# Leaving out a doubled load and moving 24 loads further back in SyncE's queue: a linear-attention block followed by a gated MLP on one core

## The chip, the cores and the metric

The kernel runs on one core of one Trainium2 chip. The metric is the device time of one execution in microseconds; the time before is the median of three runs.

## The reference

Two blocks follow one another. The first is a linear attention with a decaying state, for 4 batches, 8 heads, 768 tokens and 48 channels a head; the second is an MLP on the joined heads (3072 tokens, 384 channels, 2048 hidden).

```python
f = 1.0 / (1.0 + np.exp(-f_logit))
for t in range(S):
    state = f[:, :, t, :, None] * state + np.einsum('bhd,bhe->bhde', k[:, :, t], v[:, :, t])
    y[:, :, t] = np.einsum('bhd,bhde->bhe', q[:, :, t], state)
x = y.transpose(0, 2, 1, 3).reshape(B * S, H * D)
h = x @ w_in
g = h * (1.0 / (1.0 + np.exp(-1.702 * h)))
out = g @ w_out
```

## The kernel before

**Units.** The tokens are worked off in 12 units of 256 tokens (three units to a batch), numbered 0 to 11; "the third unit" is number 2. For each unit the kernel computes scores in six levels (distances of 1, 2, 4, ... 32 tokens inside chunks of 64), masks them into the tile A, forms the products y of A with v (line 543), adds the products of q with the carried state (line 698), copies y to yT, and lets SyncE (SP) rearrange it by DMA into xT (lines 762 and 767), the input of that unit's MLP. Between levels, f, q and k are multiplied together in the tile X (lines 528 and 532, VectorE), and ScalarE sets copies aside in Kc and Qc (lines 503 and 509). The state is updated by VectorE (lines 673 to 677), after which the products of line 698 can go on.

**Loading f, q and k.** All three have one buffer each, in the tile raw, which is used again by every unit. `load_raw(n, j)` loads f (j = 0), q (1) or k (2) of unit n. For units 0 and 1 (N_FILL is 2) it issues four loads (line 280), and the turning into X and F is done by TensorE. From unit 2 on each of f, q and k is eight DMAs (line 287), four of 96 KB and four of 80 KB, and VectorE turns them (line 354). `begin_f`, `begin` and `begin_k` turn f, q and k of a unit; `begin_f` takes a list of pieces for units 0 and 1. v is loaded by `load_v` in five DMAs (lines 306 and 311), issued in the step that forms the state of the unit before.

**Weights.** The MLP's weights are fetched in 16 pairs of 768 KB (line 208, tile bits; w_in in two DMAs, w_out in one) into three buffers in turn, and converted in steps: one activation of ScalarE (line 239) and three VectorE operations (lines 235, 228 and 238). Pairs 0, 1, 4, 5, 8, 9, 12 and 13 are w_in, the others w_out. The fetch of pair n is issued when pair n - 3 has been converted, so it waits for that pair's buffer.

**Order.** TensorE's and GpSimd's instructions stand in the order in which they are written, and up to the end of `follow(2, ...)` so do all the others. `opening()` runs unit 0 with a first part of unit 1 inside it. `parts_of(n)` gives the parts of unit n, with the beginnings of unit n + 1 put between them; `follow` goes through them and, after each, emits a planned number of MLP products, conversion steps and other chores. For unit 1 the parts are six of scores ("W"), two turnings of k ("T"), the state ("S"), its products with q ("W"), and then the beginnings of unit 2 ("B", three times). The MLP products (line 1110 for h, line 1124 for o) fill TensorE between the parts.

**SP's queue.** All loads and stores but the first four of q are issued by SP, in one order. The DMAs use eight completion semaphores in turn, so a DMA is issued only when the one eight before it has landed.

Of the kernel before, what the change touches and what calls it, by code (L numbers as in the profile page):

```python
# [23 lines left out]
def kernel(  # L24
# [52 lines left out]
    N_FILL = 2  # L77
# [32 lines left out]
    def keep_up(times, columns=(NL - 1) * 64, of=None):  # L110

        if times:
            pt = bank([P, columns], f"idle_{next(serial)}")
        for _ in range(times):
            lhs, rhs = of or (ident, masks.rearrange("p l f t -> p (l f t)"))
            nc.tensor.matmul(pt, lhsT=lhs, rhs=rhs, start=True, stop=True)
# [10 lines left out]
    R = U // 32  # L127
# [131 lines left out]
    def load_raw(n, j, engines=(nc.sync,)):  # L259
        if n >= NALL:  # L260
            return
        b, s0 = n // NU, n % NU * U
        src = (f_logit, q, k)[j]
        first = s0 - (j == 1)

        def span(head, token, dims, d=0):
            return bass.AP(src.tensor, src.offset + ((b * H + head) * S + token) * D + d, dims)
        if n < N_FILL:
            for a in range(NP):
                engine = engines[a * len(engines) // NP]  # L270
                to = by_pair[j][32 * a:32 * (a + 1), :, :R * D]
                if first < 0 and a == 0:

                    for r, rows in ((1, 16), (17, 15)):
                        engine.dma_start(
                            out=to[r:r + rows], in_=span(0, r * R - 1, [[R * D, rows], [S * D, 2], [1, R * D]])
                        )
                    engine.dma_start(out=to[:1, :, D:], in_=span(0, 0, [[R * D, 1], [S * D, 2], [1, (R - 1) * D]]))
                else:
                    engine.dma_start(out=to, in_=span(2 * a, first, [[R * D, 32], [S * D, 2], [1, R * D]]))  # L280
            return
        for f in (1, 0):
            for r in range(4):
                lo = 32 * (r % 2)
                width = R4 * D - lo
                part = span(r // 2, first + (0 if f else HALF), [[R4 * D, 32], [2 * S * D, NP], [1, width]], lo)
                nc.sync.dma_start(out=by_half[32 * r:32 * (r + 1), j, f, :, :width], in_=part)  # L287
            if f and first < 0:
                for r in range(4):
                    lo = 32 * (r % 2)  # L290
                    nc.sync.dma_start(
                        out=by_half[32 * r:32 * r + 1, j, f, :, :D - lo],
                        in_=q[b - 1, r // 2::2, S - 1:S, lo:].rearrange("a t d -> t a d"),
                    )
# [33 lines left out]
    def attention(n):  # L328
# [11 lines left out]
        parts = []  # L340
# [7 lines left out]
        def turn(j, outs, fn=None, pieces=None):  # L348

            if n >= N_FILL:  # L350
                for f in (1, 0):
                    out = outs(f)
                    at, step = (0, 1) if f else (HALF - 1, -1)
                    nc.vector.transpose(  # L354
                        view(out, at, [[HALF, NP], [step, R4], [R4 * step, 32]]),
                        by_half[:, j, f].rearrange("p a (j d) -> p (a j) d", j=R4)[:, :, :32],
                    )
                if fn:
                    fn()
                return  # L360
            for j0 in pieces or range(0, R, 4):
                pt = bank([P, 4, P], f"t_{n}_{j}_{j0}")
                for jj in range(4):
                    for h in range(2):
                        x = (j0 + jj) * D
                        nc.tensor.matmul(
                            pt[h * HS:(h + 1) * HS, jj, :], lhsT=by_pair[j][:, h, x:x + HS], rhs=ident, start=True, stop=True
                        )
                for f in (1, 0):
                    at, step = (j0, 1) if f else (HALF - 1 - j0, -1)  # L370
                    nc.scalar.activation(
                        view(outs(f), at, [[HALF, NP], [R * step, 16], [step, 4]]),
                        pt.rearrange("p j (a f i) -> p f a i j", a=NP, f=2)[:, 1 - f],
                        (AF.Tanh if n > 1 else AF.Sigmoid) if fn else AF.Copy, scale=0.5 if fn and n > 1 else 1.0,
                    )
            if fn and n > 1:
                half_up()
# [9 lines left out]
        def begin_f(pieces=None):  # L387
            def decay():
                turn(0, lambda f: F[:, ORDER.index(f) * SLOT:(ORDER.index(f) + 1) * SLOT], sigmoid, pieces)
            if n > N_FILL + 1 and "moved" in copied:  # L390
                with tc.issue_after(copied["moved"].ins):
                    decay()
            else:
                decay()
            if n >= N_FILL or (n == 1 and R - 4 in pieces):
                load_raw(n + 1, 0)

        def begin():
# [359 lines left out]
        def to_x(y, x, ng, hs=range(2)):  # L758

            for h in hs:  # L760
# [3 lines left out]
                while at < D:  # L764
# [5 lines left out]
                    at += w  # L770

        return (begin_f, begin, begin_k, begin_gates), parts, (open_level, open_evacuate, turn_k), lambda: reverse_v(n)


# [415 lines left out]
    def parts_of(n):  # L1190

        parts = list(units[n][1])
        _, inter = parts.pop()
        if n and n != N_FILL:
            kind, scores = parts[0]
            _, ahead = units[n - 1][1][-1]
            def both():
                rest = ahead()
                scores()
                if rest:  # L1200
                    rest()
            parts[0] = kind, both
        if n + 1 < NALL:
            begin_f, begin, begin_k, begin_gates = units[n + 1][0]
            i = len(parts)
            if n + 1 < N_FILL:

                parts.append(("K", lambda: (begin_k(), begin_gates())))
                kind, head = parts[0]
                parts[0] = kind, lambda: (head(), load_raw(n + 1, 1), keep_up(1))  # L1210
                parts.insert(4, ("B", lambda: (begin(), load_raw(n + 1, 2))))
                parts.insert(2, ("B", begin_f))
            else:
                kind, states = parts.pop()
                if n in CARRY:
                    parts += [("B", begin_f), ("B2", begin), ("S1", lambda: (states(), begin_gates())), ("K3", begin_k)]
                elif n < N_FILL:
                    second = parts[1][1]
                    parts[1] = parts[1][0], lambda: (second(), [load_raw(n + 1, j) for j in range(3)])
                    def own():  # L1220
                        rest = inter()
                        rest()
                    parts += [(kind, states), ("W", own), ("B", begin_f), ("B", begin), ("B", lambda: (begin_gates(), begin_k()))]
                else:
                    parts += [("B", begin_k), (kind, lambda: (states(), begin_gates()))]
                    parts.insert(i - 3, ("B", lambda: (begin_f(), begin())))
        else:
            parts.append(("W", inter))
        return parts

    def merge(n, fill, columns, share):

        parts = parts_of(n)
        total = sum(share(kind) for kind, _ in parts)
        at = done = 0
        columns += state["behind"]
        for kind, fn in parts:
            while kind in ("S", "S1") and any(in_y.get(m) for m in range(n)):
                w, emit, _ = fill.pop(0)
                emit()  # L1240
                done += w
            fn()
            at += share(kind)
            end = max(done, columns * at / total)
            while fill and done < end:
                w, emit, _ = fill.pop(0)
                emit()
                done += w
        state["behind"] = max(0, columns - done)
# [139 lines left out]
```

## Time and profile before

| | |
|---|---|
| median of three runs | 596.62 us (595.42 to 597.95) |
| span of the profiled execution | 594.2 us |
| the profiled execution's own time | not given apart from its span; the median lies 2.4 us above the span |
| TensorE (PE) busy | 566.1 us, 95% |
| VectorE (DVE) busy | 435.9 us, 73% |
| ScalarE (ACT) busy | 300.0 us, 50% |
| GpSimd (POOL) busy | 136.2 us, 23% |
| mean granted TensorE clock | 0.983 |
| DMA | 61.05 MB, mean 103 GB/s |
| loads of f of 96 KB (line 287) | 52, of 80 KB 44, the doubled load included |

The busy shares are averages over the whole span. The first 110 us, in which unit 0 and unit 1 run and the weights arrive, are the only part where the DMA load is high, where TensorE has gaps, and where its granted clock falls to half for a time; what a step there is worth is read from timelines and short windows of that part. "SPq" rows are SP's DMA issues, with the time that the issues took and not the time of the transfers.

### The profile page before, as it was taken

The page shows a single profiled execution, that of the slowest core. Times are in us where ns is not written, and L with a number is a line of the kernel's source. Part 1 is how long each engine was busy: PE and PEld are TensorE (multiplying, and loading weights), DVE is VectorE, ACT ScalarE, POOL GpSimd, SP SyncE. Part 2 cuts the span into 40 slices and gives each one's busy share as a digit, 9 for nine tenths or more (in the row PEclk, how much of TensorE's full clock was granted, in tenths as well). Part 3 has the DMA queues.
Part 4 walks back from the last instruction along what each step waited for, and adds up shares of the span by engine and source line. Part 5 has one row for each costly group of instructions (what it writes and reads, how often), then busy time and mean ns, then how long its engine had stood idle before and what let it go on. Part 6 is the DMA issues. An engine that isn't in the chain of part 4 may idle for free.

```text
span 594.2 us, 18511 instructions
## 1 busy us (share of the span) xinstructions
PE 566.1 (95%) x7820; PEld 516.0 (87%) x7820; DVE 435.9 (73%) x697; ACT 300.0 (50%) x610; POOL 136.2 (23%) x226
## 2 busy tenths in 40 slices
PE   6869897999999999999999999999999999999997
PEld 5757574768789999999999999999999999998997
DVE  2887678985979777798787797786887786461284
ACT  4854534325452575474474574563663564553440
POOL 4020020145226610610600700700600601203000
PEclk9959899999999999999999999999999999999999
DMA  7879977434452543343452243453352111001000
GB/s 186 207 183 195 242 194 180 132 79 97 115 149 60 128 110 82 93 118 98 120 137 59 76 117 86 117 147 62 93 141 63 45 55 29 28 3 27 28 1 27
DMA packets 87923, 61.05 MB, mean 103 GB/s; under 512 B 33633, under 2 KB 79617, under 8 KB 87841
## 3 DMA queue, kind: packets, MB, share of 16 engines
q1 hardware_dynamic: 87504, 59.48, 40.0%
q8 instruction: 61, 1.00, 0.7%
q10 hardware_dynamic: 337, 0.39, 0.3%
q14 instruction: 21, 0.17, 0.1%
HBM read 46.21 MB, written 8.91 MB: 93 GB/s over the span
## 4 chain that ended last, share of the span: by engine, by line
PE 81%; DVE 6%; DMA 5%; issue 3%; ACT 2%; SPq 2%; POOL 0%; DVEq 0%; ACTq 0%; POOLq 0%
PE h L1016 17%; PE o_Y L878 13%; PE o_Z L878 9%; PE h L1110 8%; PE h_y L1016 6%; PE sc L434 6%; PE o L1124 5%; PE o_X L878 5%; PE o_W L878 4%; PE y L698 2%; PE y L543 2%; SPq L287 2%; PE sc L652 2%; DMA bits<-in_moe_w_in_dram 1%; DMA raw<-in_q_dram 1%
## 5 line engine op out<-in xcount | busy, mean ns | idle before, releaser
L532 DVE TENSOR_TENSOR X<-X,tot 128x1024 f32<-128x1024 f32 x50 | 66.0, 1319 | 42.6 <-PE sc L434 38.7
L503 ACT COPY Kc<-X 128x512 f32<-128x512 f32 x72 | 48.2, 670 | 71.0 <-DVE X L532 60.1
L978 POOL TENSOR_TENSOR E<-xT 128x128 f32<-128x128 f32 (+1 forms) x36 | 18.6, 526 | 235.4 <-DMA xT<-yT 204.8
L1110 PE MATMUL h<-xT,w_in 128*128 128x256 f32 x288 | 67.2, 390 | 3.9 <-DMA xT<-yT 1.9
L1110 PEld LDWEIGHTS h<-xT,w_in 128*128 128x128 f32 x288 | 55.0, 194 | 14.0 <-issue 3.1
L1016 PE MATMUL h<-E,w_in 128*128 128x128 f32 (+1 forms) x476 | 62.5, 277 | 0.3 <-DVE g L1044 0.3
L1016 PEld LDWEIGHTS h<-E,w_in 128*128 128x128 f32 x476 | 57.3, 192 | 1.0 <-issue 0.4
L878 PE MATMUL o_Y<-T,S 128*128 128x192 f32 x320 | 57.6, 329 | 0.0
L1046 ACT ACTIVATE g<-g 128x512 f32<-128x512 f32 (+1 forms) x70 | 40.3, 589 | 26.6 <-DVE g L1044 26.6
L878 PEld LDWEIGHTS o_Y<-T,S 128*128 128x128 f32 x320 | 52.3, 190 | 0.5
L712 ACT COPY yT<-y 48x256 f32<-48x256 f32 x88 | 32.3, 367 | 31.8 <-PE y L698 30.7
L1044 DVE TENSOR_TENSOR g<-g,h 128x512 f32<-128x512 f32 (+1 forms) x58 | 36.2, 639 | 15.1 <-PE h L1016 14.1
L1124 PE MATMUL o<-w_out,g 128*128 128x384 f32 x128 | 46.6, 515 | 0.0
L354 DVE STREAM_TRANSPOSE X<-raw 128x512 f32<-128x512 f32 x40 | 42.3, 1113 | 3.1 <-PE y L698 2.7
L494 DVE COPY_PREDICATED A<-masks,sc 128x256 f32<-128x256 uint32 (+1 forms) x98 | 42.0, 505 | 0.0
L1124 PEld LDWEIGHTS o<-w_out,g 128*128 128x128 f32 x128 | 25.1, 202 | 15.8 <-issue 2.3
L434 PE MATMUL sc<-X,Kc 48*64 48x64 f32 x1344 | 30.2, 228 | 4.7 <-DVE s L228 2.3
L434 PEld LDWEIGHTS sc<-X,Kc 48*64 48x64 f32 x1344 | 25.8, 142 | 9.1 <-ACT Kc L503 4.5
L1035 ACT ACTIVATE g<-h 128x512 f32<-128x512 f32 (+1 forms) x52 | 28.5, 576 | 9.9 <-PE h L1016 9.6
L1114 ACT ACTIVATE g<-h 128x256 f32<-128x256 f32 x48 | 17.7, 382 | 30.6 <-PE h L1110 30.4
L878 PE MATMUL o_X<-w_out,g 128*128 128x192 f32 x160 | 29.9, 332 | 0.5 <-ACT o_X L842 0.5
L1044 DVE TENSOR_TENSOR g<-g,h_y 128x512 f32<-128x512 f32 (+1 forms) x29 | 18.6, 641 | 14.9 <-PE h_y L1016 10.4
(161 smaller groups left out, 1173.5 us busy)
## 6 DMA issues: line engine op xcount, KB each, us to landing
bits<-in_moe_w_out_dram SPq DMA_DIRECT2D x8, 768.0 KB, 5.4
raw<-in_f_logit_dram SPq DMA_DIRECT2D x52, 96.0 KB, 2.2
raw<-in_k_dram SPq DMA_DIRECT2D x48, 96.0 KB, 3.0
bits<-in_moe_w_in_dram SPq DMA_DIRECT2D x8, 576.0 KB, 6.1
raw<-in_q_dram SPq DMA_DIRECT2D x44, 96.0 KB, 2.3
k_tok<-z SPq DMA_DIRECT2D x64, 64.0 KB, 1.8
kt<-k_tok SPq DMA_DIRECT2D x16, 256.0 KB, 2.9
out_dram<-osb SPq DMA_DIRECT2D x20, 192.0 KB, 1.9
```

Source lines behind the costliest of these rows:

```text
L354: nc.vector.transpose(view(out, at, [[HALF, NP], [step, R4], [R4 * step, 32]]), by_half[:, j, f].rearrange("p a (j d) -> p (a j) d", j=R4) ...
L434: nc.tensor.matmul(t["sc"][h][g * HS:(g + 1) * HS, a, s, :], lhsT=t["Kc", l][rows(h), x:x + HS], rhs=rhs(h, a, g), start=True, stop=True,)
L494: moved = nc.vector.copy_predicated(out=view(A, c * HALF + at, dims), mask=mask.bitcast(U32), data=got)
L503: nc.scalar.copy(c.rearrange("p (n two m) -> p n two m", two=2, m=m), view(X, KF * SLOT, [[2 * m, SLOT // (2 * m)], [(KR - KF) * SLOT + m, ...
L532: nc.vector.tensor_tensor(x, x, y, ALU.mult)
L712: nc.scalar.copy(view(yT[rows(h)], at, [[U, NP], [step, HS]]), py[columns(h, g), g, :, f, :])
L878: nc.tensor.matmul(t[name], lhsT=lhs(f), rhs=rhs(f), start=(new and i == 0), stop=(i == HF - 1), skip_group_check=True,)
L1016: nc.tensor.matmul(ph[:, t], lhsT=WA[a][:, f * P:(f + 1) * P], rhs=E[n][b], start=(root and t == 0), stop=not goes_on, skip_group_check=True,)
L1044: nc.vector.tensor_tensor(to, to, part, ALU.add if sign > 0 else ALU.subtract)
L1046: nc.scalar.activation(to, to, AF.Gelu_apprx_sigmoid)
L1110: nc.tensor.matmul(ph, lhsT=w_in[:, c, ff * P:(ff + 1) * P], rhs=xTs[n][:, c, :], start=(c == 0), stop=(c == NK - 1))
L1124: nc.tensor.matmul(t["po"], lhsT=g[ff // FG][:, ff % FG, tt * P:(tt + 1) * P], rhs=w_out[:, ff, :], start=(ff == ffs[0]), stop=(ff == ffs[ ...
```

## The change

In the kernel before, `begin_f` of unit 1 issues the load of f of unit 2 once the second of its two pieces is turned, inside `opening()`; and `parts_of(1)` issues f, q and k of unit 2 again behind the second scores of unit 1. Unit 2's f is thus loaded twice into the same place, with the same data. The change takes the condition for unit 1 out of `begin_f`, and hangs the three loads to the fifth scores of unit 1.

```diff
             else:
                 decay()
-            if n >= N_FILL or (n == 1 and R - 4 in pieces):
+            if n >= N_FILL:
                 load_raw(n + 1, 0)
...
                 elif n < N_FILL:
-                    second = parts[1][1]
-                    parts[1] = parts[1][0], lambda: (second(), [load_raw(n + 1, j) for j in range(3)])
+                    fifth = parts[4][1]
+                    parts[4] = parts[4][0], lambda: (fifth(), [load_raw(n + 1, j) for j in range(3)])
```

On SP eight DMAs fall away, and the fetches of weight pairs 6 and 7 stand ahead of the 24 loads of f, q and k of unit 2 instead of behind them. The order on the other four engines is the same in both kernels.

## The prediction

> **What bounds the kernel now.** I read the page first, then the chain that ended last, the timelines of SP, PE and DVE from 14 to 100 us, PE's waits, and busy time with granted clock in short windows. The page gives TensorE's busy share and clock in 40 slices:
>
> ```profile
> PE   6869897999999999999999999999999999999997
> ...
> PEclk9959899999999999999999999999999999999999
> ```
>
> PE is full from the eighth slice on, so a microsecond won or lost before about 109 us reaches the end; from there to the end PE's waits in the waits view come to some 5 us. The change acts between 21 and 76 us, where PE has gaps and the clock falls to half. There SP's queue issues every load in one order. SP's timeline (start, duration, line, destination<-source, count):
>
> ```profile
> 21.32 6.84 SPq L287 DMA_DIRECT2D raw<-in_f_logit_dram  x8
> ...
> 32.02 1.05 SPq L208 DMA_DIRECT2D bits<-in_moe_w_out_dram  x1
> ...
> 41.10 7.19 SPq L287 DMA_DIRECT2D raw<-in_f_logit_dram  x8
> 48.42 4.91 SPq L287 DMA_DIRECT2D raw<-in_q_dram  x8
> 53.44 3.70 SPq L287 DMA_DIRECT2D raw<-in_k_dram  x8
> 57.23 0.90 SPq L208 DMA_DIRECT2D bits<-in_moe_w_out_dram  x2
> 58.22 6.19 SPq L208 DMA_DIRECT2D bits<-in_moe_w_in_dram  x4
> 64.50 0.39 SPq L306 DMA_DIRECT2D vt<-in_v_dram  x1
> 64.93 5.41 SPq L311 DMA_DIRECT2D vr<-in_v_dram  x4
> 70.81 0.52 SPq L762 DMA_DIRECT2D xT<-yT  x1
> ...
> 73.69 0.53 SPq L762 DMA_DIRECT2D xT<-yT  x1
> ```
>
> The load of the third unit's f is there twice, at 21.32 and 41.10; q and k follow, and only at 57.23 the two w_out fetches for weight pairs 6 and 7. Behind them come pairs 8 and 9 (58.22), the next v, and at 70.81 the rows of xT that the MLP of the second unit needs. DVE and PE, same columns:
>
> ```profile
> 62.00 0.56 DVE L235 TENSOR_SCALAR a<-bits 128x768 int32<-128x768 uint32 x1 [1.84 <-DMA bits<-in_moe_w_out_dram]
> ...
> 76.02 2.02 DVE L354 STREAM_TRANSPOSE F<-raw 128x512 f32<-128x512 f32 x2
> ```
>
> ```profile
> 39.99 2.90 PE L1110 MATMUL h<-xT,w_in 128*128 128x256 f32 x6 [1.91 <-DMA xT<-yT]
> ...
> 67.95 1.24 PE L698 MATMUL y<-X,st 48*48 48x64 f32 x58 [2.05 <-issue]
> 69.12 6.92 PE L1124 MATMUL o<-w_out,g 128*128 128x384 f32 x16
> 76.46 9.30 PE L1110 MATMUL h<-xT,w_in 128*128 128x256 f32 x42 [0.42 <-issue]
> ```
>
> DVE waits 1.84 us for pair 6. PE waits 1.91 us for the first xT and 2.05 us ahead of the y products; its products h at 76.46 start just after the xT row block issued at 73.69 can have landed (2.8 us later). Last the clock: PE busy, the third number PEld, the number behind POOL the granted clock.
>
> ```profile
> 31.20:44.80 13.60, 8.92 (x152) 7.18 (x153) 11.52 (x19) 6.84 (x14) 2.37 (x5) 0.50 0.77 191
> ...
> 68.80:72.10 3.30, 3.30 (x19) 1.94 (x8) 1.22 (x2) 2.73 (x8) 0.00 (x0) 0.50 1.24 183
> ```
>
> ```profile
> 65.40:68.70 3.30, 1.25 (x60) 0.93 (x62) 3.09 (x9) 1.17 (x2) 0.00 (x0) 1.00 1.03 226
> ...
> 27.80:31.20 3.40, 1.58 (x70) 1.31 (x68) 3.26 (x7) 2.79 (x8) 1.75 (x2) 1.00 0.90 169
> ```
>
> The clock is half after each stretch of 3.4 us in which PE was busy less than half of the time (1.25 of 3.30, 1.58 of 3.40), and it came back at 44.9 only after a full stretch.
>
> **Part 1, the first load of f goes.** Eight DMAs (four of 96 KB, four of 80 KB, 704 KB) and 6.84 us of SP's time. The order of instructions on PE, DVE, ACT and POOL is the same in both kernels; SP loses these eight and nothing else. At the 235 GB/s of the window 21 to 32 us they are 3.0 us of transfer. Who was behind them: v for the second unit (29.42), then pair 3 (32.02). Pair 3 cannot be issued earlier, since it waits for a buffer that DVE's L228 frees at 31.7; but it took 5.9 us to land, against 4.74 for the same size at 57.23 (chain view). So the xT rows behind it come up to 1.2 us earlier. Nothing is added, so no loss: bounds 0 and 1.2, I take 0.8. That start lies at half clock until 44.9, so it is worth half: **-0.4 us** (0 to -0.6). PE then runs without a wait to 59.5, so it is passed on.
>
> **Part 2, 24 loads move behind the fifth scores.** Moved past on SP: the fetches of pairs 6 and 7, nothing else; POOL issues none. Those fetches then wait only for their buffers, freed by DVE's L228 at 46.3 and 50.1. They go out there instead of at 57.23 and 57.71 and land by about 52 and 56 at 5.9 us each, before DVE asks at 60.1. Removed: DVE's 1.84. What is late next is ACT, which prepares the pair between two copies: kn ends at 60.72, the activation takes 0.93, L228 0.56, L238 0.96, so the pair is done at 63.2 instead of 64.55. The states behind it, and the y products, come 1.3 us earlier: with part 1 at 66.2 instead of 67.95.
>
> That gain meets the xT rows, which stand last in SP's queue. In the new order the raw loads start at about 50.2 (50.1 plus 0.4 for pair 7, less 0.4). Before they took 16.0 us (41.10 to 57.13). The floor is k's own pace, 3.70 for 8, so 11.1 for 24. The ceiling is 16.0 again. Of the old time, f's 7.2 held waits for pairs 4 and 5: eight transfers are in flight at once, each issue waiting for the one eight before. In the new order only f's last two stand eight behind pairs 6 and 7; I give f 4.7 (3.7 and 1.0 of that wait), q and k their old 8.7: 13.4, nearer to the floor's side because pairs 4 and 5 have landed. They end at 63.6. Pairs 8 and 9 then need 1.3 and 0.8 with gaps, so v goes out at 65.9 instead of 64.50: **+1.4** (floor -0.9, ceiling +4.0). The transfers weigh against that: the DMA share is 1.05 from 57 to 72 us, the bytes from 39 us to xT are the same in both orders, and pairs 6 and 7 now fill time before 57. Half-way, I take **+0.6** for xT, so h starts at 77.1 instead of 76.46 and the 1.7 us won at y are gone.
>
> The raw loads themselves: k lands about 66, its first reader is behind F's transposes at 76.02, ten microseconds of cover. Without it each late microsecond would be one of PE.
>
> The Trainium skill, "DMA: Bandwidth & Descriptors", section "Rules for kernel authors", says to issue a DMA early and wait for it late. It speaks against moving these loads; the trace agrees only that there is a wait to lose, and by this rule alone nothing is lost until the ten microseconds of cover are used up.
>
> Then the clock. PE's o products start at 67.5 and need 6.9 us at mostly half clock, 5.2 at full (4.68 for 14 at 49.16). They are done between 72.7 and 74.4, and PE waits 2.7 to 4.4 us for xT, where it waited 0.42. That is enough to halve the clock for one stretch as in the rows above: 3.4 us at half costs 1.7. Against it stands the half-clock stretch at 68.8, which may not come: the wait ahead of y moves to 64.2 to 66.2, across the border at 65.35, less than half of either stretch. The two about cancel at the point of h, since PE's speed ahead of a wait is worth nothing; I take +1.0 (0 to +2.7) for the clock behind h.
>
> Sum: +0.6 for xT, +1.0 for the clock, less what the later wait absorbs: PE waits 0.87 us at 108.51 for a weight pair whose DMA stands in the same SP queue and moves by 0.6 too. 0.6 plus 1.0 less 0.87 is **+0.7 us**; below the 0.6 of the queue itself it cannot fall. On the span of 594.2 that is 594.9; the median of the runs lies 2.4 above the span (596.62), and the profiled execution's own time is not given apart from its span, so 597.3.
>
> **Rivals.** *Slower: the raw block stalls SP.* If its 24 issues take the 16.0 us of before, v goes out at 68.5, and xT and the loads behind it follow 4.0 later; one stretch of half clock adds 1.7, less 0.87: +4.8 at the ceiling. With 15 us of issue it is one less, about +3.7, 600.3. SP begins to lose from 12.0 us of issue on (13.4 less the 1.4), and the loss passes half a per cent from 14.4. For it: f's 7.2 before, with the fetches now right ahead of f. Against: from 57 us the transfers seem to be the limit, not SP.
>
> The Trainium skill, "TensorE: Matmul & The Clock Gate", section "Part 1: The HAM clock gate", says that the clock drops after an idle window of about 3.4 us. Here it dropped after 2.05 us of waiting inside one stretch, so the row goes further than the page. By the page the wait ahead of h would cost no clock: this rival would be about +2.9 instead of +3.7, at the border of what can be told, and the sum +0.6 instead of +0.7.
>
> *Faster: the clock returns one stretch earlier.* If 0.8 us less waiting at 39 makes the stretch 38.0 to 41.4 count as busy, the clock returns at 41.4: 1.7 us. DVE, the buffers and pairs 6 and 7 all move with PE. With the raw block at its floor (-0.9), xT is 2.6 earlier; the stretch at 68.8 or that at 102.9 stays full, another 1.0: -3.6, so 593.0. For it: DMA is idle at 38 to 40 and PE busy from 40 on. Against: the stretch before it, with small products only, did not bring the clock back, and xT stays behind 24 issues.
>
> **How the numbers follow.** Forecast (from -1.5 to +2.5 us, 595.1 to 599.1) 0.45; slower rival 0.28; faster rival 0.27. Half a per cent, about what a measurement of this kernel can tell from no change, is 3.0 us: below 593.6 or above 599.6. So faster 0.27, same 0.45, slower 0.28. The range takes in the forecast's own and more than half of each rival, 592.8 to 600.6.
>
> **What would show it.** Right: pairs 6 and 7 issued near 46 and 50, no DVE wait for pair 6, y near 66.2, the raw block from 50.2 to 63.6, h still at 76.5 to 77.5 with PE idle ahead of it, half clock behind that. Wrong: h earlier than 75.5 (the queue did not bind), the clock back at 41.4, a raw block over 15 us, or F's transposes waiting for a DMA.

## The result and the profile after

Beside each other on one chip, the changed kernel took 599.80 us (median of 22 runs) and the kernel before 597.82 us (22 runs, one of which took 1459.35 us; the others lie between 595.11 and 599.85): a ratio of 1.0035, 95% interval 1.0023 to 1.0046, or 2.1 us more (1.4 to 2.8). The interval lies wholly above 1, so the change loses time, but less than the half per cent that the prediction counted as a difference. The profiled execution has a span of 597.4 us against 594.2, which is 3.2 us. The runs beside the experiments tell why the two sizes differ: the kernel before has a mean span of 595.45 over 85 of them, on the three chips of the experiments, so its profiled execution was a short one; the changed kernel has 597.78 over its 22. A difference read from the two traces is therefore some 0.9 us too large (3.2 against 2.3 of the means).

TensorE's busy share and clock on the page of the changed kernel:

```profile
PE   7959777999999999999999999999999999999997
...
PEclk9969979799999999999999999999999999999999
```

The sixth slice is less busy than before (7, was 9), and the clock now drops in slices 3, 6 and 8 (before in 3 and 5). What moved is seen in SP's timeline (start, duration, line, destination<-source, count):

```profile
45.88 4.18 SPq L208 DMA_DIRECT2D bits<-in_moe_w_out_dram  x2
50.16 4.61 SPq L287 DMA_DIRECT2D raw<-in_f_logit_dram  x8
55.07 4.16 SPq L287 DMA_DIRECT2D raw<-in_q_dram  x8
59.33 4.70 SPq L287 DMA_DIRECT2D raw<-in_k_dram  x8
64.13 2.51 SPq L208 DMA_DIRECT2D bits<-in_moe_w_in_dram  x4
66.74 0.43 SPq L306 DMA_DIRECT2D vt<-in_v_dram  x1
67.21 5.33 SPq L311 DMA_DIRECT2D vr<-in_v_dram  x4
72.63 0.68 SPq L762 DMA_DIRECT2D xT<-yT  x1
...
74.72 0.52 SPq L762 DMA_DIRECT2D xT<-yT  x1
```

Pairs 6 and 7 are fetched in the row at 45.88, issued at 45.88 and 49.68 instead of 57.23 and 57.71. The 24 loads fill the queue from 50.16 to 64.03, v goes out at 66.74 (before 64.50), and the second block of xT's rows at 74.72 (before 73.69): one microsecond later. VectorE and TensorE of the changed kernel, with the wait and what ended it in brackets:

```profile
70.72 0.56 DVE L235 TENSOR_SCALAR a<-bits 128x768 int32<-128x768 uint32 x1 [3.17 <-DMA bits<-in_moe_w_in_dram]
...
75.48 2.00 DVE L354 STREAM_TRANSPOSE F<-raw 128x512 f32<-128x512 f32 x2
```

```profile
39.61 2.90 PE L1110 MATMUL h<-xT,w_in 128*128 128x256 f32 x6 [2.31 <-DMA xT<-yT]
...
64.27 1.27 PE L698 MATMUL y<-X,st 48*48 48x64 f32 x64
65.47 1.56 PE L1124 MATMUL o<-w_out,g 128*128 128x384 f32 x4
67.70 4.11 PE L1124 MATMUL o<-w_out,g 128*128 128x384 f32 x12 [0.67 <-DVE w_out L238]
77.45 10.95 PE L1110 MATMUL h<-xT,w_in 128*128 128x256 f32 x42 [5.65 <-DMA xT<-yT]
...
110.87 10.85 PE L1110 MATMUL h<-xT,w_in 128*128 128x256 f32 x48
```

VectorE no longer waits for pair 6; it waits 3.17 us for pair 8, which stands behind the 24 loads. F's transposes at 75.48 wait for nothing, so the 24 loads themselves do not come too late. The y products run at 64.27 without the pause ahead of them, so the o products are done by 71.8 instead of 76.0. Then TensorE stands still for 5.65 us, because the rows of xT have not come sooner but later. The same 42 products h take 10.95 us instead of 9.30. The reason is in the windows of the changed kernel, laid on the stretches of 3.4 us in which the trace grants one clock (window, length, then busy PE, PEld, DVE, ACT, POOL, the granted clock, DMA share, GB/s):

```profile
70.55:73.95 3.40, 1.25 (x4) 0.38 (x2) 2.45 (x4) 0.92 (x1) 0.00 (x0) 1.00 1.22 213
73.97:77.37 3.40, 0.00 (x0) 0.00 (x0) 2.93 (x5) 0.91 (x1) 0.00 (x0) 0.50 0.70 137
77.40:80.78 3.38, 3.33 (x8) 2.73 (x9) 3.38 (x6) 1.44 (x2) 1.98 (x2) 0.50 0.81 281
101.30:104.65 3.35, 0.21 (x1) 0.00 (x0) 2.41 (x5) 1.95 (x5) 0.00 (x0) 1.00 1.05 229
104.70:108.10 3.40, 3.15 (x66) 2.66 (x67) 3.37 (x8) 1.46 (x2) 0.00 (x0) 0.50 0.84 239
108.10:111.50 3.40, 3.40 (x7) 1.89 (x6) 3.40 (x6) 0.10 (x1) 1.08 (x1) 0.50 0.75 235
```

PE is busy 1.25 of 3.40 us, and the next stretch is at half clock; in that one PE does nothing, so it counts against the clock again, and the first 3.3 us of h run at half. The same happens a second time at 104.7, where the kernel before lost one stretch and this one loses two.

Followed along PE, trace against trace, the loss adds up: h starts 0.99 later (77.45 against 76.46); the clock behind it adds 1.65 (10.95 less 9.30), so the scores behind it stand at 88.33 instead of 85.69; nothing changes until 104.95 against 102.29; the second half-clock stretch adds 1.17 (h at 110.87 against 107.04); the 0.87 that PE waited for a weight pair at 108.51 is absorbed. The next o products start at 121.55 against 118.56: 2.99 us, and from there to the end, where the spans differ by 3.2, little is added.

### The profile page after: what moved, and what is told of

It is laid out like the page before. It is cut to its first block, busy times and chain, and to the rows that moved or that the text cites. A ratio compares the mean times of both kernels' runs of the same rounds, so it can differ in the third digit from the quotient of the medians.

```text
span 597.4 us, 18507 instructions
## 1 busy us (share of the span) xinstructions
PE 565.9 (95%) x7820; PEld 516.6 (86%) x7820; DVE 435.6 (73%) x697; ACT 299.7 (50%) x610; POOL 136.2 (23%) x226
## 4 chain that ended last, share of the span: by engine, by line
PE 81%; DVE 8%; DMA 4%; ACT 3%; issue 2%; SPq 1%; DVEq 0%; ACTq 0%
PE h L1016 16%; PE o_Y L878 13%; PE h L1110 10%; PE o_Z L878 9%; PE h_y L1016 6%; PE sc L434 6%; PE o L1124 5%; PE o_X L878 5%; PE o_W L878 4%; DMA bits<-in_moe_w_in_dram 2%; PE y L543 2%; PE y L698 2%; PE sc L652 2%; DVE X L532 2%; DVE X L354 1%
## 5 line engine op out<-in xcount | busy, mean ns | idle before, releaser
L1110 PE MATMUL h<-xT,w_in 128*128 128x256 f32 x288 | 68.5, 396 | 8.7 <-DMA xT<-yT 8.0
L1110 PEld LDWEIGHTS h<-xT,w_in 128*128 128x128 f32 x288 | 56.4, 198 | 19.0 <-issue 9.3
L1124 PEld LDWEIGHTS o<-w_out,g 128*128 128x128 f32 x128 | 24.4, 196 | 16.1 <-ACT yT L712 1.3
L1114 ACT ACTIVATE g<-h 128x256 f32<-128x256 f32 x48 | 18.1, 385 | 35.2 <-PE h L1110 35.0
L878 PE MATMUL o_W<-T,g 128*128 128x192 f32 x160 | 29.5, 331 | 0.0
```

What stands on the lines that cost most here:

```text
L878: nc.tensor.matmul(t[name], lhsT=lhs(f), rhs=rhs(f), start=(new and i == 0), stop=(i == HF - 1), skip_group_check=True,)
L1110: nc.tensor.matmul(ph, lhsT=w_in[:, c, ff * P:(ff + 1) * P], rhs=xTs[n][:, c, :], start=(c == 0), stop=(c == NK - 1))
L1124: nc.tensor.matmul(t["po"], lhsT=g[ff // FG][:, ff % FG, tt * P:(tt + 1) * P], rhs=w_out[:, ff, :], start=(ff == ffs[0]), stop=(ff == ffs[ ...
```

## The experiments

Ratios are to the kernel before, run beside it on the same chip (medians of it: 597.70 for the first four, 597.00 for the next four, 597.43 for the last two). A ratio is estimated from all the runs, with its 95% interval, and need not be the quotient of the two medians: for the eighth run that would be 0.9972. Each run left one profile, of one execution.

**Each half alone.** The first run takes only the doubled load away; the loads stay behind the second scores.

```diff
-            if n >= N_FILL or (n == 1 and R - 4 in pieces):
+            if n >= N_FILL:
```

> Only the doubled load of f goes; f, q and k stay behind the second scores. Theory (the later place of the 24 loads costs the time, by making the second unit's xT rows later, and the missing load is worth little): -0.4 us against the kernel before, within 0 to -1.2; h of the second unit starts at 76.0 to 76.5 us and PE waits less than 1 us ahead of it. Rival (the missing load itself costs, by shifting the opening against the clock's stretches): +1.5 to +2.5 us, with h at about 76.5 and a longer time at half clock in the first 45 us.

Measured: 598.31 us, 1.0005 (0.9989 to 1.0020): no difference. Its h on PE's timeline:

```profile
76.67 9.30 PE L1110 MATMUL h<-xT,w_in 128*128 128x256 f32 x42 [2.56 <-DMA xT<-yT]
```

The wait of 2.56 us was not expected: TensorE's o products were done by 74.1 instead of 76.0, since they ran at full clock, and the rows came as late as before. Yet the clock stays full behind this wait.

The second run moves the loads and keeps the doubled one.

```diff
-                    second = parts[1][1]
-                    parts[1] = parts[1][0], lambda: (second(), [load_raw(n + 1, j) for j in range(3)])
+                    fifth = parts[4][1]
+                    parts[4] = parts[4][0], lambda: (fifth(), [load_raw(n + 1, j) for j in range(3)])
```

> The doubled load stays in the opening; f, q and k go behind the fifth scores. Theory: +2.0 to +3.2 us against the kernel before (the whole loss of the change and the 0.4 of the missing load on top); the 24 issues run from about 50.5 to 64.5 us, v for the third unit goes out at 66.5 to 67.5, h starts at 77 to 78.5 after a PE wait of 4 to 6 us. Rival (the missing load costs): -0.5 to +0.5.

Measured: 599.79 us, 1.0038 (1.0024 to 1.0053), with the same picture on PE as the whole change:

```profile
77.48 10.99 PE L1110 MATMUL h<-xT,w_in 128*128 128x256 f32 x42 [5.68 <-DMA xT<-yT]
```

So the loss is the move's. This run also takes away the evidence for the removal's small gain: the first unit's h starts at 39.50 in it, with the doubled load still there, and at 39.61 with the load gone.

**What the wait costs: the queue or the clock.** Back to the changed kernel; the third run moves v of unit 2 behind the rows of xT, so that these no longer stand behind five loads.

```diff
+            if n != 1:
                 load_v(n + 1)
...
                         rest()
+                        load_v(n + 1)
```

> The changed kernel with the five loads of the third unit's v issued behind the second unit's xT rows instead of ahead of them. Theory (SP's order makes the rows late): the first row goes out when yT is ready, at 67 to 68 us instead of 72.6, lands behind the fetch of pair 9 at 74 to 75, h starts at 74.5 to 75.5 instead of 77.45, the PE wait falls to 2.5 to 3.5 us, and half clock lasts 3.4 us or less there: -2 to -3.5 us against the changed kernel, so -1.5 to +0.5 against the kernel before. Rival (the transfers alone bound the rows, whatever the order): h at 77 and +2.0 as the changed kernel.

Measured: 597.84 us, 1.0005 (0.9989 to 1.0021). SP issues the first rows at 67.53 instead of 72.63. PE's h:

```profile
75.77 12.14 PE L1111 MATMUL h<-xT,w_in 128*128 128x256 f32 x42 [3.61 <-DMA xT<-yT]
```

Five microseconds at the issue became 1.7 at h, since the rows landed only from 74.9 on, behind pair 9 (74.68). So the queue's order is a part of the lateness, and the transfers already under way seem to be the rest. And h took 12.14 us, because two stretches at half clock followed, of which only the first microsecond (from 74.70) lay in the wait. The profiled execution took 598.90 us, 1.1 more than the median of the run, so it shows one of the dearer cases.

The fourth run leaves the queue alone and keeps TensorE from standing still: seven products of constants, into a bank that nobody reads, ahead of h (they do not enter the result).

```diff
+        for _ in range(7):
+            nc.tensor.matmul(pt, lhsT=ident, rhs=masks.rearrange("p l f t -> p (l f t)"), start=True, stop=True)
+        emit()
```

> The changed kernel with seven matmuls on constants, into a bank that nobody reads, put ahead of the second unit's first h, so that PE is busy while it waits for the xT rows. Theory (the clock is part of the cost): h starts where it did, 77.3 to 78, but at full clock, its first 42 matmuls take 9.3 us instead of 10.95; -1.2 to -1.8 us against the changed kernel, so +0.2 to +1.0 against the kernel before. Rival (only the lateness of the rows counts): +1.8 to +2.2 against the kernel before.

Measured: 598.40 us, 1.0016 (0.9998 to 1.0033). PE (a product in two matmuls, so x14):

```profile
70.87 3.93 PE L1341 MATMUL idle<-masks,ident 128*128 128x320 f32 x14
77.09 9.30 PE L1110 MATMUL h<-xT,w_in 128*128 128x256 f32 x42 [2.29 <-DMA xT<-yT]
```

The rows come at 77.09, only 0.36 us sooner than in the changed kernel; 9.30 us is the full clock again, and the scores behind stand at 86.33, 2.0 us sooner. The o products behind the later wait start at 119.90, 1.65 us sooner (121.55). In time the run gives back 0.0022 of the 0.0038 of the moved loads on the same chip, some 1.3 us; the intervals overlap, so the trace shows this split and the times only agree with it; the granted clocks of all the runs, given further down, bear it out.

**Is the fifth place the wrong one?** The fifth run hangs the loads to the fourth scores, so that pair 6 alone goes ahead of them; the sixth adds five products of constants to that.

```diff
-                    fifth = parts[4][1]
-                    parts[4] = parts[4][0], lambda: (fifth(), [load_raw(n + 1, j) for j in range(3)])
+                    fourth = parts[3][1]
+                    parts[3] = parts[3][0], lambda: (fourth(), [load_raw(n + 1, j) for j in range(3)])
```

> The changed kernel with the 24 loads behind the fourth scores: the fetch of pair 6 stands ahead of them, that of pair 7 behind. Theory (what counts is when SP gets to pairs 8 and 9 and v, whose transfers stand ahead of the xT rows): the block is issued from about 46.4 to 60.5 us, v goes out at 63 to 64 against 66.7 in the changed kernel, h of the second unit starts at 74 to 75.5 after a PE wait of 2 to 4 us; -1.5 to +0.5 us against the kernel before. Rival (the loss grows with how far back the loads stand, as a question of their own landing): between the two kernels, +0.7 to +1.5.

> As e5_fourth, with five matmuls on constants ahead of the second unit's first h. Theory: h starts as in e5_fourth, at full clock; another -0.5 to -1.7 us, so -2.5 to -0.5 against the kernel before. If a later wait is the bound instead (the weight pair that PE waited for at 108.51 in the kernel before), it equals e5_fourth within 0.3 and that wait grows.

Measured: 598.69 us, 1.0028 (1.0010 to 1.0046), and 597.16 us, 1.0005 (0.9991 to 1.0019). The expected gain came in neither: the sixth, forecast at -2.5 to -0.5 us, measured +0.3. In the fifth the loads end at 61.33, but now pair 7 is behind them and late, and h stands at 78.19. PE of the fifth run, then of the sixth:

```profile
69.45 5.80 PE L1124 MATMUL o<-w_out,g 128*128 128x384 f32 x12 [3.30 <-DVE w_out L238]
78.19 9.30 PE L1110 MATMUL h<-xT,w_in 128*128 128x256 f32 x42 [2.94 <-DMA xT<-yT]
```

```profile
67.42 4.11 PE L1124 MATMUL o<-w_out,g 128*128 128x384 f32 x12 [1.14 <-DVE w_out L238]
...
75.49 9.30 PE L1110 MATMUL h<-xT,w_in 128*128 128x256 f32 x42 [1.27 <-DMA xT<-yT]
```

A wait of 3.30 us for pair 7 halved the clock ahead of h (5.80 us for what takes 4.11), and the 2.94 us ahead of h did not. In the sixth, h starts at 75.49, but the constant products did not bring it forward: they stand behind the o products, and these already waited only 1.14 us, since the loads had ended at 59.24. SP's order is the same in both runs, so two executions of one order can differ by 2.7 us at h, and a smaller difference between two single traces proves little. The 0.99 us that the move costs at h rests on two traces on either side: 77.45 and 77.48 with it, 76.46 and 76.67 without. What the sixth had won at h was gone at the o products behind the later wait (118.79, before 118.56), after half clock from 100.47 to 107.29.

**If the rows come early, who is next?** The seventh run is the kernel before without the doubled load, its 24 loads behind the second scores, and v behind the rows as in the third run.

> The doubled load goes, f, q and k stay behind the second scores, and the third unit's v is issued behind the second unit's xT rows. Theory (rows bound by the transfers of pair 9, and the time of the end by the weight pair waited for at 108.51, whose SP queue does not move): rows go out at 69.5 to 70.5, h starts at 73.5 to 74.8 instead of 76.67 without any PE wait of over 1 us, but the later wait of PE on the weights grows from 0.9 to 2 or 3 us, so that only -0.3 to -1.2 us is left against the kernel before. Rival (what is won at h is kept): -2 to -3.

Measured: 599.94 us, 1.0047 (1.0030 to 1.0064): a loss of 2.8 us where a small gain was expected, and the slowest of all. PE:

```profile
72.98 9.30 PE L1111 MATMUL h<-xT,w_in 128*128 128x256 f32 x42 [0.57 <-DMA xT<-yT]
...
108.52 12.62 PE L1111 MATMUL h<-xT,w_in 128*128 128x256 f32 x46 [4.34 <-DVE w_in L238]
```

The rows bring h 3.5 us forward, and all of it is gone at 108.52, the very time of the kernel before (108.51): the wait there for a weight pair has grown from 0.87 to 4.34, since pairs 12 and 13 are fetched from the same queue and no sooner (issue from 96.45 to 98.31, before from 95.59 to 98.31); VectorE, which converts them, waits 2.41 and 0.72 us for these transfers. A longer wait was expected; that it would take all, and then halve the clock (from 106.64 to 113.47), so that h takes 12.62 instead of 10.21, was not.

**The loads in another queue.** The eighth run is the changed kernel with the 24 loads issued by GpSimd, which has nothing else to do at that time.

```diff
-                nc.sync.dma_start(out=by_half[32 * r:32 * (r + 1), j, f, :, :width], in_=part)
+                (nc.gpsimd if n == N_FILL else nc.sync).dma_start(
+                    out=by_half[32 * r:32 * (r + 1), j, f, :, :width], in_=part
+                )
```

> The changed kernel with the 24 loads issued by GpSimd instead of SP. Theory (SP's issue of the block, 13.9 us, holds up pairs 8 and 9): pair 8 goes out at 53 us, pair 9 at 61, v right behind, h starts at 73 to 76; -2 to 0 us against the kernel before. Rival (the transfers are the limit and the issue is not): pairs 8 and 9 go out earlier, but the rows land as before and h starts at 77 to 78; +1.5 to +2.5 against the kernel before.

Measured: 595.31 us, 0.9958 (0.9941 to 0.9975). GpSimd, SP and PE:

```profile
35.31 5.11 POOL L287 DMA_DIRECT2D raw<-in_f_logit_dram  x8
...
57.61 0.55 POOL L287 DMA_DIRECT2D raw<-in_k_dram  x1 [0.80 <-DMA raw<-in_q_dram]
```

```profile
55.03 0.84 SPq L208 DMA_DIRECT2D bits<-in_moe_w_in_dram  x2
...
62.39 0.83 SPq L208 DMA_DIRECT2D bits<-in_moe_w_in_dram  x2
```

```profile
75.76 9.30 PE L1112 MATMUL h<-xT,w_in 128*128 128x256 f32 x42 [2.02 <-DMA xT<-yT]
```

The loads go out from 35.31 to 58.2, wherever they hang in the program (GpSimd has no other instruction from 35.2 to 78.45, so hung to the second scores its order would be the same). The run thus changes two things, the queue and the time of the loads; which of them counts for more was not tested. SP fetches pair 8 at 55.03, not at 64.13, VectorE waits for no transfer of a weight pair between 58 and 77 us, and h stands at 75.76 at full clock. The ninth run gives GpSimd one more block, k of unit 3, which in SP's queue stands right ahead of pairs 12 and 13. The tenth moves only this k to GpSimd, on top of the seventh.

```diff
+                (nc.gpsimd if n == N_FILL or (n == N_FILL + 1 and j == 2) else nc.sync).dma_start(
```

> As e8_pool_issues, and the eight loads of the fourth unit's k are issued by GpSimd too. Theory (PE's wait on a weight pair at 107 to 109 us is set by SP's queue, which runs without a break from 76 to 98 us): pair 13 goes out at 93.5 to 95 instead of 97, PE's wait of 0.9 goes, h starts at 106.5 to 107.3 instead of 107.83; -0.5 to -1.5 us against e8_pool_issues, so -3 to -4 against the kernel before. Rival (that wait is set by the transfers or by VectorE's order): equal to e8_pool_issues, -2.5 against the kernel before.

> As e7_remove_v_behind, with the eight loads of the fourth unit's k issued by GpSimd. Theory (e7 lost at 108.5 us, on the weight pair behind the fourth unit's loads in SP's queue, what it had won at h): pair 13 goes out at 92 to 94.5 instead of 97.4, PE's wait of 4.3 us there falls below 1.5, half clock behind it to one stretch or none; -2.5 to -5 us against e7_remove_v_behind, so -2.2 to +0.3 against the kernel before. Rival (e7 was slow for another reason, such as v coming later): within 1 us of e7_remove_v_behind, +2 to +3.

Measured: 594.49 us, 0.9943 (0.9924 to 0.9962), and 596.56 us, 0.9984 (0.9967 to 1.0002). PE of the ninth run:

```profile
74.07 9.30 PE L1112 MATMUL h<-xT,w_in 128*128 128x256 f32 x42
...
104.71 10.87 PE L1112 MATMUL h<-xT,w_in 128*128 128x256 f32 x48
```

and of the tenth:

```profile
107.68 10.22 PE L1113 MATMUL h<-xT,w_in 128*128 128x256 f32 x46 [0.34 <-DVE w_in L238]
```

In the ninth both waits are gone, the one for xT and the one for pair 13. The first is not the doing of its edit: GpSimd issues k of unit 3 only at 82.52, after h has started at 74.07, so this is the spread between executions again. The second fits the edit, as SP now fetches pairs 12 and 13 from 89.80 on (94.63 in the eighth). The ninth version is faster than the kernel before. Its lead over the eighth is within the intervals and was not measured on one chip. The tenth differs from the seventh by 0.006 with intervals apart, and its wait at 107.68 is 0.34 us instead of 4.34; but its h had also come 2.3 us later (75.28), and TensorE was ready for the weight pair at 107.34 instead of 104.18. So 3.2 us of the shorter wait are this lateness, and 0.8 the pair that came sooner.

## Why the prediction was right, and where its sizes were off

The forecast was 0.7 us above the time before; it is 2.1 us above, inside the forecast's own bounds (-1.5 to +2.5) and the range. The direction was right, and the size a third of what was measured. The mechanism was the one named: the gain at y is eaten by the rows of xT behind the raw block, and the wait ahead of h costs clock. By its steps:

- **Part 1 (-0.4, 0 to -0.6).** Alone it measured +0.3 us (-0.7 to +1.2): no gain seen, none excluded.
- **Pairs 6 and 7** were to be issued near 46 and 50: 45.88 and 49.68. No wait of VectorE for pair 6, as said. That pair 8 would be late by 3.17 us was not in the prediction; it cost nothing in this trace, since h waited longer for xT.
- **y at 66.2** was mis-sized: it is 64.27. The pause of 2.05 us went wholly, not by 1.3 us, and TensorE had come 0.9 us early to that point (o at 48.22, before 49.16), as the long stretch at half clock ended at 43.2 instead of 44.9. That is a shadow of the faster rival, but not its condition: the stretch came later and was shorter, and did not end at 41.4. Nor does its length follow either half of the change: it is 6.8 or 10.2 us in the traces of all ten runs, with the doubled load still there (second) or the loads in their old place (first, seventh, tenth), and 13.7 only in that of the kernel before. The 3.7 us won at y are worth nothing, as the prediction said of the 1.7 it counted on.
- **The raw block, 13.4 us from 50.2 to 63.6:** 13.9 us, to 64.03. **v +1.4:** +2.24. **h +0.6, half-way:** +0.99, at 77.45 for 77.1. Halving the queue's delay at h came out near enough, 2.24 at v became 0.99, but it was a choice half-way between two readings, so this is luck in part.
- **The wait ahead of h, 2.7 to 4.4 us:** 5.65, because y came sooner than forecast and the clock was full ahead of it.
- **The clock behind h (+1.0, 0 to +2.7)** is the mis-sized term: 1.65 in the trace. The 0.7 taken off the 1.7 of one stretch, because that at 68.8 might not come, was wrong, since that stretch lies ahead of the wait and is worth nothing whether it comes or not. A second term was missing: the stretch at 102.9 that the kernel before has became two, another 1.17. A wait of 3.42 us ahead of the scores is there in both kernels; shifted against the stretches, it left 0.21 us of work in one (0.61 before), and the next, with 3.15 us busy, did not bring the clock back. This term follows no order of the loads: two stretches stand there in the traces of the changed kernel and of the second, fifth, sixth and tenth run, one in those of the kernel before and of the first, third, fourth, seventh, eighth and ninth. So in the fourth run, where both terms are gone, only the first is shown to be the constant products' doing. Its later wait is 1.59 us, where the changed kernel has none and the kernel before 0.87.
- **The 0.87 absorbed at 108.51** went as forecast.

With its sizes put right the sum is 0.99 + 1.65 + 1.17 - 0.87 = 2.94, the traces' 2.99: that is one pair of traces added up, not a second measurement, and the runs say 2.1. How the two clock terms stand in other executions can only be bounded: from the granted clock of the runs (twice what is missing to 1, times the span), the kernel before spent a mean of 16.1 us at half clock (85 runs), the changed one 21.1 (22 runs). These 5.0 us cost 2.5 at most, and less where they fall into a wait. On the chip of the first four runs the means are 15.4 us for the kernel before (30 runs), 19.3 for the move alone (7) and 14.9 with the constant products (12): filling the wait takes the added half clock away over all the runs, and not only in the profiled one.

The slower rival named the raw block at over 14.4 us; it took 13.9, and its loss of a microsecond per microsecond of issue did not come: half of it was lost. (At 15 us of issue its own terms give 3.0 plus 1.7 less 0.87, that is 3.8 and not 3.7.) Its second half, one stretch of clock behind h, did. For that the prediction held two readings against each other. "TensorE: Matmul & The Clock Gate" in the Trainium skill, section "Part 1: The HAM clock gate", asks for an idle window of about 3.4 us; here the clock fell at 73.97 after a stretch with 1.25 us of work in it, as the row has it. The half clock that h paid, from 77.40, does not decide between the two: it follows a stretch without any work. The rule of the Trainium skill, "DMA: Bandwidth & Descriptors", section "Rules for kernel authors", to issue early, fits here only where the earlier transfer does not stand ahead of a more urgent one: the fetches of pairs 6 and 7 went out earlier, and pair 8 and the rows of xT later for it. The eighth run issues the 24 loads earlier than either kernel and gains, by a queue that nobody else uses at that time.

## What to carry to other kernels

In one queue a load has no price of its own: it costs what it delays behind it, so moving a block to relieve one wait lets the next one out, and the last in the queue (here the rows of xT, then the weight pair) decides. Before such a move, write down every transfer behind the block with its reader's time; if another engine is free to issue, give it the bulk. And count a wait twice, once as time and once for the clock behind it: of the waits of 3.30 and 2.94 us in the fifth run only the first cost clock as well, 1.7 us (5.80 instead of 4.11).

## What the runs showed of the chip that was not expected

Waits of 2.56, 2.29, 2.94 and 2.02 us ahead of h (first, fourth, fifth and eighth run) cost no clock, while 2.05 (before, ahead of y), 3.30, 3.61, 4.34 and 5.65 us did. In these traces the time at half clock in the first 120 us comes in multiples of 3.41 us: 10.24 (33.00 to 43.24) and twice 6.83 (73.96 to 80.79, 104.68 to 111.51) in the changed kernel. So what counts is how a wait lies to the borders of these stretches: that of 2.05 us lay inside one, that of 2.94 us (75.25 to 78.19) across the border at 76.30. The prediction's border, half of a stretch busy, fits most rows but not all. In the changed kernel, the tenth and the fifth run:

```profile
29.60:33.00 3.40, 1.89 (x99) 1.60 (x89) 3.33 (x5) 2.05 (x6) 2.97 (x4) 1.00 0.03 7
```

```profile
65.55:68.96 3.41, 1.83 (x66) 1.45 (x64) 3.24 (x8) 1.57 (x4) 0.00 (x0) 1.00 1.03 236
```

```profile
76.30:79.71 3.41, 1.52 (x7) 1.40 (x8) 3.41 (x5) 1.06 (x1) 0.57 (x1) 1.00 0.55 123
```

The clock was half behind the first two, with TensorE busy for more than half of the stretch, and stayed full behind the third, with less. In the first all products are small ones with an output of 48x64 or 64x64, in the second 64 of 66; in the third all are 128x256. Small products may thus count for less than their time; no run placed a wait or chose the products on purpose, and the border stays open. So does the way back: a stretch at half clock with 3.15 of 3.40 us busy (66 products, 64 of them small) did not bring the full clock back, and one with 3.04 us (eighth run, 40.72 to 44.12, 14 products) did.

Rows issued five microseconds sooner let h start only 1.7 us sooner (third run), and they landed behind pair 9, fetched ahead of them: the queue's order alone does not set when a transfer lands.
